# Two dense layers by Strassen's scheme, over 1024 rows and from weight sums kept in DRAM, with the stages in sequence

## The chip, the core and the metric

One NeuronCore of one Trainium2 chip runs the kernel. The metric is the device time of one launch in microseconds (us); the time of a kernel is the median of its runs. Five engines run their own queues in order: TensorE (PE in the profile; PEld is its loading of weights), VectorE (DVE), ScalarE (ACT), GpSimd (POOL), and SyncE (SP), which here only issues transfers between DRAM and SBUF. PSUM is the memory into which PE writes, in banks of 512 float32 per partition.

## What is computed

`x` holds 2048 rows of 576 float32. Two layers with the same weights: attention with learned features, then two dense layers with a squared ReLU between them (576 to 4608 to 576).

```python
q, k, v = heads(layernorm(x) @ wqkv)               # 32 heads of 18
phi_q = concat(softmax(q @ w_phi), softmax(-(q @ w_phi)))   # phi_k alike, per head
o = phi_q @ (phi_k.T @ v) / (phi_q @ phi_k.sum() + 1e-6)
x = x + o @ wo
h = relu(layernorm(x) @ w1 + b1) ** 2
x = x + h @ w2 + b2
```

Nothing in it is causal: the sums over the keys run over all 2048 rows, so no row's attention can end before every row's keys are done. Both kernels keep float32 accuracy in the large products by splitting each operand into a high and a low part (float32r) and adding three products of parts; `w_phi` is folded into `wqkv`.

## The kernel before

The rows are cut into four blocks of 512. For a block, `g_mlp` runs over 36 chunks of 128 hidden features. A chunk's slices of w1 and w2 are loaded from the inputs (288 KB each, and again for each block and layer), rounded to their high parts on ACT (L588, L591) and their low parts taken on DVE (L589, L592; a rest of 64 columns on POOL, L593). Fourteen products of 512 columns make the chunk's hidden rows in one PSUM bank (L605); ACT applies the bias, ReLU and square (L611, L612), DVE splits the result (L615, L616), and fourteen more products add to the output, which stays in five PSUM banks over all 36 chunks (L634, L627). The second products of a chunk are issued a step after its hidden ones, so that PE has work while ACT and DVE make the operands.

Attention is written as generators. `weave` takes one step of the dense layers of a block, then a step or two of the attention of the next block (`g_back`: norm, projections, softmax, the features over their denominators, the attention's output, its norm). The steps stand in this order in the program, and a list scheduler fixes from it the order of each engine's queue. Attention's own operations: max and min per head (L353, L354), two subtractions, one on DVE (L357) and one on POOL (L358), exp (L359), sums and reciprocals (L361, L362); for keys a product on POOL (L369). For queries `g_phi` takes the denominators: a product by the sums of the keys (L493), its sum per head (L494), a reciprocal (L497), a product (L501). `g_out` transposes the features (L521), splits them (L522, L523), multiplies by the key sums (L535), splits the result (L537, L539), multiplies by `wo` (L558) and adds to the rows (L561). `g_norm` is L245 to L278.

Two stretches in each layer have no dense products to weave with: the first layer's keys (with the fold before them), and the barrier, where the last keys end the sums and one block's attention runs alone before its dense layers can start.

Of the kernel before, what the change touches and what calls it, by code (L numbers as in the profile page):

```python
# [14 lines left out]
TB = 512  # L15
NT = TB // P
# [5 lines left out]
def layers_kernel(  # L22
# [24 lines left out]
    NB = S // TB  # L47
    NF = F // P
    KC = D // P                      # full blocks of 128 features
    DT = D - KC * P                  # the features beyond  # L50
    assert DT * 2 == P
# [4 lines left out]
    gw = [min(GW, D - g * GW) for g in range(NG)]  # L56
    HP = D // 2                      # 288

    cst = ctx.enter_context(tc.tile_pool(name="cst", bufs=1))
    sb = ctx.enter_context(tc.tile_pool(name="sb", bufs=2))  # L60
    ps_w = ctx.enter_context(tc.tile_pool(name="ps_w", bufs=2, space=bass.MemoryType.PSUM))
    ps_a = ctx.enter_context(tc.tile_pool(name="ps_a", bufs=1, space=bass.MemoryType.PSUM))
    dram = ctx.enter_context(tc.tile_pool(name="dram", bufs=1, space=bass.MemoryType.DRAM))

    xs = [[dram.tile([P, D], F32, name=f"xs{b}_{t}") for t in range(NT)] for b in range(NB)]
    xm = [[dram.tile([P, D], F32, name=f"xm{b}_{t}") for t in range(NT)] for b in range(NB)]
    xth = [dram.tile([P, NC * TB], F32, name=f"xth{b}") for b in range(NB)]
    xtl = [dram.tile([P, KC * TB], F32, name=f"xtl{b}") for b in range(NB)]
    wf = dram.tile([D, 2 * D], F32, name="wf")

    # Work tiles in PSUM: two banks at all times; the banks of the dense layers too while these rest.
    spare = {"tags": [], "i": 0}

    def wtile(name):
        n = len(spare["tags"])
        spare["i"] += 1
        i = spare["i"] % (n + 2)
        if i < n:
            return ps_a.tile([P, TB], F32, tag=spare["tags"][i], name=name)
        return ps_w.tile([P, TB], F32, tag="w", name=name)  # L80

    def drain(gen):
        for _ in gen:
            pass

    def weave(main, other, rate):
        """main's steps with other's between them, rate of these to one; then the rest of other."""
        due = 0.0
        for _ in main:
            due += rate  # L90
            while due >= 1.0 and next(other, other) is not other:
                due -= 1.0
        drain(other)

    def lagged(n, produce, consume):
        """consume(i, produce(i)) for all i, each a step behind, so that no engine waits for the other."""
        held = None
        for i in range(n):
            new = produce(i)
            if i:  # L100
                consume(i - 1, held)
            held = new
            yield
        consume(n - 1, held)
        yield

# [17 lines left out]
    zeros = zero.unsqueeze(1).to_broadcast([1, TB // P, P])  # L124
    mhalf = cst.tile([P, 1], F32, name="mhalf")
    nc.vector.memset(mhalf, -0.5)
    b1t = cst.tile([P, NF], F32, name="b1t")
# [6 lines left out]
    def rows_twice(src, c0, n):  # L134
        """The last DT rows of src, columns c0.., on both halves of the partitions."""
        w = src.shape[1]
        return bass.AP(tensor=src.tensor, offset=src.offset + KC * P * w + c0,
                       ap=[[0, 2], [w, DT], [1, n]])

    TAGS_A = ("whi", "wlo")  # L140
    TAGS_B = ("s2", "h1")

# [1 line left out]
    def g_fold(kpair):  # L144
        """Makes wf, and of it the pieces for k at once."""
        phi = sb.tile([P, NC, P], F32, tag="r1", name="phi")[:GW, :NG, :GW]
# [7 lines left out]
        raws, folds = {}, {}  # L154

        def turn(k):
            c, i = divmod(k, 3)
            if i == 0:
                raws[c] = sb.tile([P, 2 * D], F32, tag="E", name=f"fr{c}", bufs=4)
                nc.sync.dma_start(raws[c], wqkv[c * P : (c + 1) * P, : 2 * D] if c < KC  # L160
                                  else rows_twice(wqkv, 0, 2 * D))
                folds[c] = sb.tile([P, 2 * D], F32R, tag="hb", name=f"ff{c}").bitcast(F32)
            w, n = gw[batches[i][0][1]], len(batches[i])
            pt = wtile(f"fp{c}_{i}")
            for j, (h, g) in enumerate(batches[i]):
                a = h * D + g * GW
                nc.tensor.transpose(pt[:w, j * P : (j + 1) * P], raws[c][:, a : a + w], ident)
            wt = sb.tile([P, TB], F32, tag="hr", name=f"ft{c}_{i}", bufs=2)
            nc.vector.tensor_copy(wt[:w, : n * P], pt[:w, : n * P])
            return wt  # L170

        def times(k, wt):
            c, i = divmod(k, 3)
            w, n = gw[batches[i][0][1]], len(batches[i])
            folded = folds[c]
# [4 lines left out]
            keys = []  # L180
            if i < 2:
                nc.scalar.activation(folded[:, i * D : i * D + n * w], po[:, : n * w], AF.Copy)
                if i == 1:
                    keys = [(0, 0, HP, 0), (1, 0, n * w - HP, HP)]
            else:
                nc.scalar.activation(folded.rearrange("p (h d) -> p h d", h=2)[:, :, last * GW :],
                                     po[:, : 2 * w].rearrange("p (h d) -> p h d", h=2), AF.Copy)
                keys = [(1, last * GW - HP, w, w)]
            for half, to, width, at in keys:
                hi, lo = (piece[:, c, to : to + width] for piece in kpair[half])  # L190
                nc.scalar.activation(hi, po[:, at : at + width], AF.Copy)
                nc.vector.tensor_sub(lo, po[:, at : at + width], hi.bitcast(F32))
            if i == 2:
                m = P if c < KC else DT
                nc.sync.dma_start(wf[c * P : c * P + m, :], folded[:m])

        yield from lagged(3 * NC, turn, times)

# [1 line left out]
    def piece_tiles(name, tags):  # L200
        return [sb.tile([P, NC * HP], F32R, tag=tag, name=f"{name}{n}").rearrange("p (c n) -> p c n", c=NC)
                for tag, n in zip(tags, "hl")]

    def wpiece(src, c0, name, tags=TAGS_A, heads=False):
# [13 lines left out]
        for p, c in parts:  # L218
            nc.scalar.activation(hi[p, c], raw[p, c], AF.Copy)
            nc.vector.tensor_sub(lo[p, c], raw[p, c], hi[p, c].bitcast(F32))  # L220
# [596 lines left out]
```

## Time and profile before

| what | value |
|---|---|
| time, median of 3 runs | 2693.22 us (2692.66 to 2694.44) |
| profiled execution, first to last instruction | 2693.9 us |
| busy: PE, DVE, ACT, POOL | 2614.6, 1574.4, 1065.3, 605.8 us |
| products and transposes on PE | 13364 |
| mean granted clock of PE | 0.989 |
| DRAM traffic | 280.26 MB, 104 GB/s over the span |
| instructions | 36380 |

The profile gives, for one execution, each engine's busy time; the 40 equal slices of the span (busy tenths, the clock granted to PE in tenths, DMA share); the chain of work that ended last; and groups of instructions by line, engine and shape with their busy time, the mean length of one in ns, and the idle time before them with what ended it. A window gives the busy times of a stretch. Lengths of PE's products overlap, since they are pipelined; the step from one to the next is read from starts.

### The profile page before, as it was taken

What the parts mean: (1) busy time and instruction counts of PE and PEld (TensorE: products, weight loads), DVE (VectorE), ACT (ScalarE), POOL (GpSimd) and SP (SyncE); (2) the same over time, 40 slices, a digit from 0 to 9 for tenths busy, and PEclk for the clock granted to TensorE, in tenths of its full rate; (3) what the DMA queues carried; (4) which work ended last, traced back from release to release, by engine and by line L of the source; (5) the groups of instructions that cost most, each with busy time, mean ns of one, the idle gap of its engine ahead of it and who ended that gap; (6) DMA issues with size and microseconds to landing.
All of it is one profiled execution on the core that took longest, in us unless ns stands there. A gap on an engine that the chain in (4) does not pass through costs nothing. (4 is left out here: it accounts for less than half of the span.)

```text
span 2693.9 us, 36380 instructions
## 1 busy us (share of the span) xinstructions
PE 2614.6 (97%) x13364; PEld 2211.8 (82%) x13364; DVE 1574.4 (58%) x2561; ACT 1065.3 (40%) x1837; POOL 605.8 (22%) x647
## 2 busy tenths in 40 slices
PE   6998999999999999999999989999999999999998
PEld 5997788888878888788888977888888887888887
DVE  5668944365764567547544688444854476444343
ACT  3334343344433444434443333434434343433433
POOL 1443411112311123112211333111321123111110
PEclk8998999999999999999999989999999999999999
DMA  6211233352333532334333113333432343234332
GB/s 208 89 32 45 74 110 101 98 180 84 109 112 97 171 110 82 112 97 132 113 95 109 43 57 114 87 100 102 154 118 86 102 160 97 84 101 128 98 97 74
DMA packets 289021, 280.26 MB, mean 104 GB/s; under 512 B 18697, under 2 KB 230153, under 8 KB 286793
## 3 DMA queue, kind: packets, MB, share of 16 engines
q1 hardware_dynamic: 288841, 277.92, 34.0%
q8 instruction: 105, 1.72, 0.3%
q14 instruction: 75, 0.61, 0.1%
HBM read 246.90 MB, written 30.97 MB: 103 GB/s over the span
## 5 line engine op out<-in xcount | busy, mean ns | idle before, releaser
L605 PE MATMUL m_0ph<-a_0nh,m_0h 128*128 128x512 f32 (+1 forms) x760 | 231.6, 387 | 0.0
L605 PE MATMUL m_2ph<-a_2nh,m_2h 128*128 128x512 f32 (+1 forms) x760 | 228.2, 383 | 0.1
L634 PE MATMUL m_3acc<-m_3s,m_3hb 128*128 128x512 f32 x864 | 214.2, 395 | 3.0 <-DVE m_3hb L616 1.8
L634 PE MATMUL m_0acc<-m_0s,m_0hb 128*128 128x512 f32 x864 | 214.7, 395 | 2.5 <-DVE m_0hb L616 1.1
L634 PE MATMUL m_1acc<-m_1s,m_1hb 128*128 128x512 f32 x864 | 213.3, 394 | 2.6 <-DVE m_1hb L615 1.8
L634 PE MATMUL m_2acc<-m_2s,m_2hb 128*128 128x512 f32 x864 | 213.2, 394 | 0.9 <-DVE m_2hb L615 0.7
L634 PEld LDWEIGHTS m_0acc<-m_0s,m_0hb 128*128 128x128 f32 x864 | 161.0, 188 | 43.4 <-DVE m_0hb L616 4.2
L634 PEld LDWEIGHTS m_3acc<-m_3s,m_3hb 128*128 128x128 f32 x864 | 160.9, 188 | 43.1 <-DVE m_3hb L616 4.2
L634 PEld LDWEIGHTS m_1acc<-m_1s,m_1hb 128*128 128x128 f32 x864 | 161.3, 188 | 42.1 <-DVE m_1hb L615 3.2
L634 PEld LDWEIGHTS m_2acc<-m_2s,m_2hb 128*128 128x128 f32 x864 | 161.3, 188 | 40.3 <-DVE m_2hb L615 2.2
L605 PEld LDWEIGHTS m_0ph<-a_0nh,m_0h 128*128 128x128 f32 x760 | 141.0, 190 | 28.5 <-DVE m_0h L589 0.4
L605 PEld LDWEIGHTS m_2ph<-a_2nh,m_2h 128*128 128x128 f32 x760 | 139.6, 188 | 28.8 <-DVE m_2h L589 1.0
L589 DVE TENSOR_TENSOR m_2h<-m_2r,m_2h 128x640 fp32r<-128x640 f32 x72 | 61.5, 854 | 165.4 <-ACT m_2h L588 165.4
L589 DVE TENSOR_TENSOR m_1h<-m_1r,m_1h 128x640 fp32r<-128x640 f32 x72 | 61.0, 848 | 162.5 <-ACT m_1h L588 162.5
L589 DVE TENSOR_TENSOR m_3h<-m_3r,m_3h 128x640 fp32r<-128x640 f32 x72 | 60.8, 844 | 160.8 <-ACT m_3h L588 160.8
L589 DVE TENSOR_TENSOR m_0h<-m_0r,m_0h 128x640 fp32r<-128x640 f32 x72 | 62.7, 870 | 145.9 <-ACT m_0h L588 139.2
L593 POOL TENSOR_TENSOR m_3s<-m_3r,m_3s 128x64 fp32r<-128x64 f32 x72 | 57.3, 797 | 355.2 <-ACT m_3s L591 349.6
L593 POOL TENSOR_TENSOR m_2s<-m_2r,m_2s 128x64 fp32r<-128x64 f32 x72 | 55.9, 777 | 360.9 <-ACT m_2s L591 355.4
L593 POOL TENSOR_TENSOR m_1s<-m_1r,m_1s 128x64 fp32r<-128x64 f32 x72 | 58.0, 805 | 343.8 <-ACT m_1s L591 341.7
L593 POOL TENSOR_TENSOR m_0s<-m_0r,m_0s 128x64 fp32r<-128x64 f32 x72 | 53.3, 741 | 346.3 <-ACT m_0s L591 323.8
L611 ACT ACTIVATE m_0hr<-m_0ph,b1t 128x512 f32<-128x512 f32 x72 | 49.6, 689 | 193.9 <-PE m_0ph L605 184.7
L611 ACT ACTIVATE m_3hr<-m_3ph,b1t 128x512 f32<-128x512 f32 x72 | 49.7, 690 | 192.4 <-PE m_3ph L605 187.8
(1527 smaller groups left out, 6949.8 us busy)
## 6 DMA issues: line engine op xcount, KB each, us to landing
m_3r<-in_B_w SPq DMA_DIRECT2D x72, 288.0 KB
m_2r<-in_B_w SPq DMA_DIRECT2D x72, 288.0 KB
m_0r<-in_B_w SPq DMA_DIRECT2D x72, 288.0 KB
m_1r<-in_B_w SPq DMA_DIRECT2D x72, 288.0 KB
m_3r<-in_B_w SPq DMA_DIRECT2D x72, 256.0 KB
m_2r<-in_B_w SPq DMA_DIRECT2D x72, 256.0 KB
m_0r<-in_B_w SPq DMA_DIRECT2D x72, 256.0 KB
m_1r<-in_B_w SPq DMA_DIRECT2D x72, 256.0 KB
```

The lines of the kernel that those rows point to most:

```text
L589: nc.vector.tensor_sub(l1, r1, h1.bitcast(F32))
L593: nc.gpsimd.tensor_sub(s2[:, D : D + DT], r2[:, R:], s2[:, R:D].bitcast(F32))
L605: nc.tensor.matmul(ph[:, cols], a, m, start=(k == 0), stop=(k == 3 * KC + 1))
L611: nc.scalar.activation(hr, ph, AF.Relu, bias=b1t[:, f : f + 1])
L634: nc.tensor.matmul(acc[t], a[:, rows], m, start=(begin and k == 0), stop=(end and k == 2))
```

## The change

The dense layers work on superblocks of 1024 rows, two for each layer, and by Strassen's scheme in Winograd's form: rows, hidden features and model features are each cut in two, and seven products of half-size blocks stand for eight. The hidden layer takes a pair of chunks at a time (`NJ` = 18 pairs): seven products of weight sums with row sums, each seven matmuls of 512 columns (L585), over three PSUM banks, with additions on DVE (L603 to L618) that put together the four blocks of the result. The second layer takes two pairs of chunks at a time: for each of seven products, operands are made of the four hidden blocks (POOL, L631 to L637; split by ACT and DVE, L639, L640), and four tiles of 128 rows by 288 columns are made in PSUM, six matmuls each (L657), and added into SBUF (L661). At a superblock's end `combine` (L671 to L693) adds the seven results into four blocks and the rows.

The weight sums are made and split once and put into DRAM: `prep_w1` (L359 to L379), one pair of chunks with each tile of the first layer's keys and two more at its end; `prep_w2` (L381 to L399) in the first superblock's dense stage. The split projection weights go to DRAM too. `norm2` makes the seven row sums on POOL and splits them (L511 to L533).

`weave` is gone. Each layer is a stage of keys for all 16 tiles (norm, v, k and q, both softmaxes, the sums; the exponentials of q go to DRAM), and for each superblock `stage_q` (the rest of the attention) and `stage_mlp`.

```diff
+    def prep_w1(pl, j):
...
+        s4, s1, s2, s3 = ws[:, 2], ws[:, 4], ws[:, 5], ws[:, 6]
+        nc.gpsimd.tensor_add(s1, a21, a22)
+        nc.gpsimd.tensor_sub(s3, a11, a21)
+        nc.gpsimd.tensor_sub(s2, s1, a11)
+        nc.gpsimd.tensor_sub(s4, a12, s2)
+        wt = pl.tile([P, 7, 5, P], F32R, tag="wt", name=f"wt{j}")
+        nc.scalar.activation(wt[:, :, :3], ws[:, :7], AF.Copy)
+        nc.vector.tensor_sub(wt[:, :, 3:], ws[:, :7, :2], wt[:, :, :2].bitcast(F32))
...
+        nc.sync.dma_start(w1d[j], wt.rearrange("p a b c -> p (a b c)").bitcast(F32))
+
...
+            def hidden(j):
...
+                def product(p, bank, fresh):
+                    w = pl.tile([P, 5, P], F32R, tag="w1", name=f"{n}w{j}_{p}", bufs=6)
+                    nc.sync.dma_start(w.rearrange("p b m -> p (b m)").bitcast(F32),
+                                      w1d[j][:, p * 5 * P : (p + 1) * 5 * P])
+                    k = 0
+                    for l, r in ((0, 0), (0, 3), (3, 0), (1, 1), (1, 4), (4, 1), (2, 2)):
+                        nc.tensor.matmul(bank, w[:, l], X[:, p, r], start=(fresh and k == 0), stop=(k == 6),
+                                         skip_group_check=not fresh)
+                        k += 1
+
...
+                a, b, c = banks
+                product(0, a, True)
+                nc.scalar.activation(p1, a, AF.Copy)
+                product(5, b, True)
+                nc.vector.tensor_add(u2, b, p1)
+                product(1, a, False)
...
+            def operand(j, p):
...
+                nc.scalar.activation(t[:, 0], o[p], AF.Copy)
+                nc.vector.tensor_sub(t[:, 1], o[p], t[:, 0].bitcast(F32))
+                return t
+
...
+            def second(js, first, final):
+                for p in ORDER2:
+                    parts = []
+                    for j in js:
+                        w = pl.tile([P, 2, HP], F32R, tag="w2", name=f"{n}v{j}_{p}", bufs=5)
+                        nc.sync.dma_start(w.rearrange("p k n -> p (k n)").bitcast(F32),
+                                          w2d[j][:, p * 2 * HP : (p + 1) * 2 * HP])
+                        parts.append((operand(j, p), w))
+                    for t in range(4):
+                        rows = slice(t * P, (t + 1) * P)
+                        pt = wtile(f"{n}y{js[0]}_{p}{t}")[:, :HP]
+                        k, last = 0, 3 * len(parts) - 1
+                        for hl, w in parts:
+                            for x, y in ((0, 0), (0, 1), (1, 0)):
+                                nc.tensor.matmul(pt, hl[:, x, rows], w[:, y], start=(k == 0), stop=(k == last))
+                                k += 1
+                        to = acc[:, p, t]
+                        if not first:
+                            nc.vector.tensor_add(to, pt, to)
+                        elif p in (1, 3):
+                            nc.vector.tensor_add(to, pt, b2t[:, :HP])
...
+            hidden(1)
+            for g in range(NJ // G):
+                if prep:
+                    for j in range((g + 2) * G, min((g + 3) * G, NJ)):
+                        prep_w2(pl, j)
+                if (g + 1) * G < NJ:
+                    hidden((g + 1) * G)
+                second([g * G + k for k in range(G)], g == 0, g == NJ // G - 1)
+                if (g + 1) * G + 1 < NJ:
+                    hidden((g + 1) * G + 1)
+            combine()
...
-            weave(g_mlp(layer, b, ready, rows, f"m{n}"), g_back(), 1.0 if layer else 1.5)
...
+                xT = lead.pop(0)
+                vt = make_v(pl, xT, wts["v"], f"v{layer}{t}")
+                kraw = make_raw(pl, xT, wts["k"], f"k{layer}{t}")
+                qraw = make_raw(pl, xT, wts["q"], f"Q{layer}{t}")
+                if held:
+                    kv_tile(banks, *held, False)
+                held = (vt, soft_k(pl, kraw, f"K{layer}{t}"))
+                soft_q(pl, qraw, layer, t, f"s{layer}{t}")
+                if layer == 0:
+                    prep_w1(pl, t)
+                    if t >= NT - 2:
+                        prep_w1(pl, t + 2)
+            kv_tile(banks, *held, True)
+            kv_end(pl, layer, banks)
+        with pool(f"px{layer}") as px:
+            X = px.tile([P, 7, 5, TW], F32R, tag="X", name=f"X{layer}")
+            for sb in range(NSB):
+                if sb:
+                    X = px.tile([P, 7, 5, TW], F32R, tag="X", name=f"X{layer}{sb}")
+                stage_q(layer, sb, X)
+                stage_mlp(layer, sb, X)
```

Where instructions move, the order of the engines shows it. First VectorE in the first layer's keys. Before (`K_2_1` is a key tile, `n_3` the norm of the next block):

```order
170 L353 TENSOR_REDUCE K_2_1m<-k_2s_1490 128x32
171 L354 TENSOR_REDUCE K_2_1m<-k_2s_1490 128x32
172 L267 TENSOR_TENSOR n_3l<-n_3p_1538,n_3h 128x4x128
173 L357 TENSOR_TENSOR K_2_1e<-k_2s_1490,K_2_1m 128x576
174 L250 TENSOR_SCALAR n_3n_1641<-x_3_2_1631,n_3m_1634,n_3d_1635 128x512
175 L361 TENSOR_REDUCE K_2_1r<-K_2_1e 128x64
176 L362 RECIPROCAL K_2_1r<-K_2_1r 128x64
177 L353 TENSOR_REDUCE K_2_2m<-k_2s_1598 128x32
```

and after (`K010` and `s010` are the softmaxes of K and Q of tile 10, `wt` the split w1 sums):

```order
261 L266 TENSOR_REDUCE K010m<-k010s 128x32
262 L267 TENSOR_REDUCE K010m<-k010s 128x32
263 L270 TENSOR_TENSOR K010e<-k010s,K010m 128x576
264 L273 TENSOR_REDUCE K010r<-K010e 128x64
265 L274 RECIPROCAL K010r<-K010r 128x64
266 L375 TENSOR_TENSOR wt_2499<-ws_2486,wt_2499 128x7x256
267 L266 TENSOR_REDUCE s010m<-Q010s 128x32
268 L267 TENSOR_REDUCE s010m<-Q010s 128x32
```

A key tile's softmax stood next to the norm of a later block; now the split of the w1 sums (L375), which waits for ACT and POOL, stands between the softmax of K and that of Q.

Second, VectorE in the dense layers. Before, in the first chunks of a block (`m_0h`, `m_0s` split weights, `m_0hb` the split hidden rows):

```order
1866 L589 TENSOR_TENSOR m_0h_2_16850<-m_0r_2_16845,m_0h_2_16850 128x640
1867 L615 CAST m_0hb_16724<-m_0hr_16721 128x512
1868 L616 TENSOR_TENSOR m_0hb_16724<-m_0hr_16721,m_0hb_16724 128x512
1869 L589 TENSOR_TENSOR m_0h_3_16930<-m_0r_3_16925,m_0h_3_16930 128x640
1870 L615 CAST m_0hb_16744<-m_0hr_16741 128x512
1871 L616 TENSOR_TENSOR m_0hb_16744<-m_0hr_16741,m_0hb_16744 128x512
1872 L592 TENSOR_TENSOR m_0s_2_16853<-m_0r_2_16846,m_0s_2_16853 128x512
```

and after, inside the second layer of a superblock (`m11hl` the split operands, `m11acc` the seven results in SBUF, `m11y` a tile in PSUM):

```order
2896 L640 TENSOR_TENSOR m11hl_4_25296<-m11s_25248,m11hl_4_25296 128x512
2897 L661 TENSOR_TENSOR m11acc<-m11y_60_25262,m11acc 128x288
2898 L640 TENSOR_TENSOR m11hl_4_25301<-m11s_25256,m11hl_4_25301 128x512
2899 L661 TENSOR_TENSOR m11acc<-m11y_61_25270,m11acc 128x288
2900 L661 TENSOR_TENSOR m11acc<-m11y_62_25278,m11acc 128x288
2901 L661 TENSOR_TENSOR m11acc<-m11y_63_25286,m11acc 128x288
2902 L640 TENSOR_TENSOR m11hl_5_25339<-m11s_25248,m11hl_5_25339 128x512
2903 L661 TENSOR_TENSOR m11acc<-m11y_40_25304,m11acc 128x288
```

Splitting of weights is gone from the stream; in its place stand the additions of PSUM tiles, four for each of the seven products, with the next product's operands split between them.

Third, TensorE. Before, in the dense layers (`m_2` is a block's dense layers, `v_3` the v projection of another block's keys):

```order
2306 L308 MATMUL v_3pv_5600<-w_3v1h,n_3h 128x288
2307 L308 MATMUL v_3pv_5600<-w_3v1l,n_3h 128x288
2308 L605 MATMUL m_2ph_5630<-a_2nh,m_2h_5_5623 128x512
2309 L605 MATMUL m_2ph_5630<-a_2nl,m_2h_5_5623 128x512
2310 L605 MATMUL m_2ph_5630<-a_2nh,m_2h_5_5623 128x512 x2
2311 L605 MATMUL m_2ph_5630<-a_2nl,m_2h_5_5623 128x512
```

and after, at the end of the first superblock's dense stage (`m00y` its last output tiles, `q_0apt` the transposes of the next stage's attention):

```order
1204 L657 MATMUL m00y_22_9048<-m00v_2_9020,m00hl_2_9023 128x288 x3
1205 L657 MATMUL m00y_22_9048<-m00v_2_9026,m00hl_2_9029 128x288 x3
1206 L657 MATMUL m00y_23_9056<-m00v_2_9020,m00hl_2_9023 128x288 x3
1207 L657 MATMUL m00y_23_9056<-m00v_2_9026,m00hl_2_9029 128x288 x3
1208 L451 MATMUL q_0apt_9202<-ident,q_00e 126x128
1209 L451 MATMUL q_0apt_9211<-ident,q_00e 126x128
```

Where projections of another block stood between two chunks, the dense products now run to their end, and the next superblock's attention begins behind them.

More of the change, by code (lines that the diff above doesn't have):

```diff
@@ L63, in layers_kernel @@
+    psa = ctx.enter_context(tc.tile_pool(name="psa", bufs=1, space=bass.MemoryType.PSUM))
     dram = ctx.enter_context(tc.tile_pool(name="dram", bufs=1, space=bass.MemoryType.DRAM))
[L65 to L68, printed above, removed]
@@ L69, in layers_kernel @@
-    wf = dram.tile([D, 2 * D], F32, name="wf")
-    spare = {"tags": [], "i": 0}
-    def wtile(name):
[L75 to L93, printed above, removed]
@@ L189, in times @@
[L189 to L202, printed above, removed]
@@ L314, in make_v @@
+    def make_v(pl, xT, w, name):
+        vt = pl.tile([P, NG, GW + 1], F32, tag="v", name=f"{name}v", bufs=3)
         nc.gpsimd.memset(vt[:, :, 0:1], 1.0)
[L315 to L328 removed]
@@ L398, in kv_tile, with kv_begin, bank_view @@
+    def kv_begin(layer):
+        banks = [abank(i, f"kv{layer}{i}") for i in range(len(pairs))]
+        for pt, gs in zip(banks, pairs):
+            m = gw[gs[0]] + 1
+            nc.tensor.matmul(pt[:m], zero[:, :m], zeros, start=True, stop=False)
+        return banks
+    def bank_view(pt):
+        return pt[: GW + 1, : 4 * GW].rearrange("p (g s f) -> p g s f", g=2, s=2)
+    def kv_tile(banks, vt, e, last):
+        for pt, gs in zip(banks, pairs):
+            po = bank_view(pt)
             for g in gs:
```

919 lines of the change are left out of this document (414 added, 505 removed).

## Prediction

> **What bounds the kernel now.** I read the page first (busy shares, the 40 slices), then the chain of waits, then windows over single stages, then the groups by shape for the price of each operation. The page:
>
> ```profile
> span 2693.9 us, 36380 instructions
> PE 2614.6 (97%) x13364; PEld 2211.8 (82%) x13364; DVE 1574.4 (58%) x2561; ACT 1065.3 (40%) x1837; POOL 605.8 (22%) x647
> PEclk8998999999999999999999989999999999999999
> ```
>
> TensorE (PE) is busy for 97% of the span at full clock nearly throughout; VectorE (DVE) has 42% to spare. The span is 0.7 us over the median of the runs (2693.22), so a sum against the span needs no correction. The chain gives the pace of the products:
>
> ```profile
> 2366.12 3.98 PE a_2po L558 x30
> 2370.11 3.18 PE m_3ph L605 x14
> ...
> 2404.96 3.17 PE m_3ph L605 x14
> 2408.14 2.79 PE m_3acc L634 x12
> 2410.93 0.47 PE m_3acc L627 x2
> 2411.39 3.26 PE m_3ph L605 x14
> ```
>
> From 2404.96 to 2411.39 there are 28 products of 512 columns, 0.230 us each; from 2366.12 to 2370.11 there are 30 of 288 columns, 0.133 each. (The durations in the groups overlap; these are the steps from one to the next.) The windows tell what each stage is like, columns as headed: length, busy time of PE, PEld, DVE, ACT, POOL, clock, DMA share, GB/s:
>
> ```profile
> 0.00:52.80 52.80, 29.84 (x175) 25.72 (x176) 29.59 (x72) 16.59 (x35) 5.50 (x22) 0.81 0.58 207
> 30.00:45.00 15.00, 6.59 (x28) 5.93 (x29) 8.14 (x16) 6.35 (x13) 0.19 (x1) 0.50 0.58 212
> 52.80:61.40 8.60, 8.60 (x67) 8.60 (x67) 4.46 (x14) 2.88 (x12) 2.15 (x5) 1.00 0.94 218
> 140.70:181.00 40.30, 40.30 (x288) 39.29 (x287) 23.83 (x31) 14.25 (x35) 15.87 (x13) 1.00 0.06 15
> 235.00:301.00 66.00, 57.32 (x371) 51.46 (x370) 61.11 (x110) 25.00 (x45) 26.94 (x27) 0.91 0.16 51
> 500.00:700.00 200.00, 198.62 (x1029) 168.66 (x1028) 115.33 (x180) 84.66 (x147) 39.10 (x46) 1.00 0.44 134
> ```
>
> In the woven part (500 to 700) PE is full while DVE does 115 of 200 us: the attention of the next block rides under the dense products. Where attention stands alone (235 to 301, four tiles of 128 rows of the barrier) DVE is busy 61.1 of 66 us and PE's clock falls to 0.91. So attention by itself is paced by DVE, and the weave is what hides that. The change takes the weave away; that decides my forecast.
>
> **The products: the gain.** Before: 36 chunks x 28 x 4 blocks x 2 layers = 8064 products of 512 columns, x 0.230 = 1855 us. After: four superblock stages of 18 x 49 = 882 hidden products of 512 (3528, 811 us) and 18 x 84 = 1512 second products of 288 (6048, 804 us): 1615. PE's work falls by 240 us. "TensorE: Matmul & The Clock Gate" of the Trainium skill (section "Back-to-back issue gap") gives N/2.4 + 2.5 ns, which is 216 and 122.5 ns, and would put these products at 1502 us as an estimate; the measured steps above are longer, and decide.
>
> **The second layer's additions.** Its output no longer gathers in PSUM: per pair of chunks DVE adds 28 tiles of 288 into SBUF and splits 14 operands of 512. The nearest rows:
>
> ```profile
> L616 DVE TENSOR_TENSOR m_1hb<-m_1hr,m_1hb 128x512 fp32r<-128x512 f32 x72 | 51.9, 720 | 2.2
> L592 DVE TENSOR_TENSOR m_0s<-m_0r,m_0s 128x512 fp32r<-128x512 f32 x72 | 60.2, 837 | 36.0 <-ACT m_0s L591 34.1 <-DMA m_0r<-in_B_w 1.9
> L561 DVE TENSOR_TENSOR a_2x<-a_2po,a_2x 128x288 f32<-128x288 f32 x16 | 7.3, 457 | 11.2 <-PE a_2po L558 11.1
> L267 DVE TENSOR_TENSOR n_3l<-n_3p,n_3h 128x512 fp32r<-128x512 f32 x8 | 5.5, 687 | 0.6 <-ACT n_3h L266 0.5
> ```
>
> 168 products take PE 22.4 us. By the order of the changed kernel 28 additions and 11 of the splits stand beside them: 28 x 0.457 + 11 x 0.72 = 20.7 us, about 22 with some 0.03 us between instructions: a tie with PE. The other 3 splits and the 10 additions of 512 (about 0.69 by L267) lie under the two hidden groups (2 x 49 x 0.230 = 22.5 us) with room. A pair costs PE 45.0 us; I take 46.5, one and a half for the tie. Bounds 45 (PE alone) and 50 (splits at L592's price and POOL's four combinations per chunk in the way). Nine pairs, four stages: 1674 us, from 1620 to 1800. That the weights come split from DRAM takes ACT and DVE work off (L588, L589, L592); it buys nothing by itself, since it lay under PE. The loads, 295 or 328 KB for each 1.6 us of PE, need some 200 GB/s; 218 is shown at a share of 0.94 in the window from 52.8, with smaller packets. I cost them at nothing, because five or six buffers run ahead; uncovered, they are in the upper bound.
>
> **First layer's keys, with the preparation of w1.** Before, a tile of keys took 40.3 / 4 = 10.1 us, PE full. After, Q's projections and softmax join each tile, and one of 18 preparations of w1. Its tiles are single, and in DVE's order its split (L375) stands between K's and Q's softmax; on POOL the product that normalises K's features stands ahead of three of the preparation's four sums. So a tile is one chain through three in-order queues. The rows for it:
>
> ```profile
> L494 DVE TENSOR_REDUCE a_2u<-a_2m 128x32 f32<-128x576 f32 x16 | 11.6, 733 | 0.0
> L357 DVE TENSOR_TENSOR K_1e<-k_0s,K_1m 128x576 f32<-128x576 f32 x1 | 1.4, 1398 | 0.0
> L357 DVE TENSOR_TENSOR K_2e<-k_1s,K_2m 128x576 f32<-128x576 f32 x1 | 0.8, 842 | 0.0
> L361 DVE TENSOR_REDUCE K_2r<-K_2e 128x64 f32<-128x1152 f32 x3 | 4.0, 1350 | 0.1
> L362 DVE RECIPROCAL K_2r<-K_2r 128x64 f32<-128x64 f32 x3 | 1.7, 553 | 0.0
> L220 DVE TENSOR_TENSOR a_0q0l<-a_0q0r,a_0q0h 128x1440 fp32r<-128x1440 f32 x1 | 1.7, 1659 | 0.6 <-ACT a_0q0h L219 0.6
> L588 ACT ACTIVATE m_2h<-m_2r 128x640 fp32r<-128x640 f32 x72 | 52.5, 729 | 3.7 <-DMA m_2r<-in_B_w 3.6
> L359 ACT ACTIVATE K_2e<-K_2e 128x1152 f32<-128x1152 f32 x3 | 3.5, 1169 | 0.7 <-DVE K_2e L357 0.7
> L593 POOL TENSOR_TENSOR m_3s<-m_3r,m_3s 128x64 fp32r<-128x64 f32 x72 | 57.3, 797 | 355.2 <-ACT m_3s L591 349.6 <-issue 5.6
> L369 POOL TENSOR_TENSOR K_2e<-K_2e,K_2r 128x1152 f32<-128x1152 f32 x3 | 6.5, 2154 | 3.9 <-DVE K_2r L362 3.9
> ```
>
> A softmax is max and min (2 x 0.73), the subtraction (1.4), exp (1.17), sum (1.35), reciprocal (0.55): 5.9 us, for K and Q 11.8. Between them: POOL's product 2.15; three sums of 384, between 0.8 (64 wide) and 1.2 (on the line from 64 to 1152), I take 1.0: 3.0; ACT's rounding of 2688 elements, on the line through 640 and 1152, 2.5; L375, 1792 wide, 2.0 by L220's price for an element. That is 9.7. One of the two small splits L378 (896 wide, 1.05 by the same price) shows, the other lies under Q's exp; a dozen hand-offs between engines at some 0.1 make 1.4. Together 24 us a tile; 20 if the sums overlap K's product and a hand-off is free, 26 with all POOL work at its slower price. On SP the store of each prepared tile waits for that DVE work, with later loads behind it; x has three buffers, which cover it. 16 x 24 = 384, plus a start like the 52.8 us of before (50, as one tile is normed ahead instead of four), plus 35 for two preparations left over and the sums' end: 469 (395 to 521).
>
> **Second layer's keys.** No preparation: 84 projections x 0.133 + sums and transposes, 13 us of PE a tile, against 12 of DVE by the same rows with the norm's. Close enough to collide: 14.5. 16 x 14.5 = 232, plus some 30 before the first tile is through, for three weights, 8.8 MB together, that SP issues only behind the previous stage's stores (at the 218 GB/s of the window from 52.8 they take 41; PE's first tile wants the last of them only after some 9): 262 (240 to 290).
>
> **The attention alone, four times.** Per tile on DVE: two reductions 1.46, one product of 576, two and a half splits of 512 from PSUM 1.7, the output's splits 0.9, two additions 0.9, statistics and norm 2, half of the operands' split (1792 and 896 wide) 1.5, the small ones 1.3:
>
> ```profile
> L501 DVE TENSOR_TENSOR a_0Q0e<-a_0Q0e,a_0Q0r 128x576 f32<-128x576 f32 x2 | 3.4, 1721 | 0.0
> L501 DVE TENSOR_TENSOR a_2Q1e<-a_2Q1e,a_2Q1r 128x576 f32<-128x576 f32 x2 | 2.9, 1428 | 0.0
> ```
>
> With 1.5 for the product: 11.3 us, so 90 for eight tiles. Nothing hides the head (loads behind the stores of the stage before, then POOL's products) nor the tail (four POOL combinations, a rounding, two splits, ahead of the first hidden product): 8 and 10. With another 10 for waits in order, 118 a stage, 472 for four; bounds 98 (no waits, half of the ends hidden) and 140 (the 15 us a tile of the barrier window, and the ends). Q's features go through DRAM, 0.62 MB a tile; I cost that at nothing, since three and four buffers let it run ahead (at 218 GB/s it is 2.9 us a tile; uncovered, it is in the upper bound).
>
> **The rest.** Combining a superblock: 32 additions of 288 on DVE, 14.6 us, all ahead of the next stage's first DVE instruction: 55 for the four (40 to 75; some lie under the last products). w2's preparation in the first stage alone: 36 halves with single tiles on POOL and DVE (about 2 us of DVE per chunk, in a tie already): 50 (15 to 110).
>
> **Sum**: 469 + 262 + 472 + 1674 + 55 + 50 = 2982 us, 288 over the span.
>
> **The rivals.** (1) *The engines overlap as before; the end is faster.* The queues would run far enough ahead of each other for PE to set the pace in keys and attention too. What is not dense products costs 2694 - 1855 = 839 us now; with 1620, combination 55 and 50 of preparation that is 2565. For it: the 40.3 us of keys with PE full. Against it: the barrier window, where the same attention left PE 9 us idle in 66. It decides if a first-layer keys tile takes under 14 us and an attention stage under 75. Half-way mixtures are still over 2694: the keys and the attention would have to give back 288 of 469 + 472 us. Chance 0.07.
>
> (2) *The second layer is set by DVE and POOL.* If POOL's combinations block DVE, 28 additions cost not 0.457 but about 0.76 (the ratio of L357's 1398, beside POOL's L358, to its 842): 8.4 us a pair, 36 pairs, 300 more: 3282. Against it: L561's 16 calls average 457, as its other groups do. "SBUF — State Buffer" of the Trainium skill (section "Who interferes with whom") says that a VectorE instruction with at most one SBUF input does not contend with GpSimd, one with two does; by that the additions from PSUM are safe and only the splits suffer, as L561 and L357 have it. Chance 0.12.
>
> (3) *The clock.* In 30 to 45 us, with PE busy 6.6 of 15, the clock is 0.50. With PE idle half of a tile in the first keys and a third of the attention, its bursts would run at half speed: PE's 13 us a tile then become up to 26, over the chain's 24 (+32), and attention tiles go from 11 to about 14 (+95): 3110. "TensorE: Matmul & The Clock Gate" of the Trainium skill (section "What's actually happening") has the clock halved after an idle window of about 3.4 us and freed after as long a busy one; bursts here are longer than that, so by the rule they lose 1.7 us each and hardly the whole. Chance 0.07, inside the range.
>
> **How the numbers follow.** The forecast has 0.74. Its terms' bounds, taken as independent, give -130 and +180 (roots of the summed squares): 2850 to 3160. With half-way mixtures below and rival 3 above, the range is 2835 to 3165; left out are rival 1, most of 2, and the forecast's tails. A measurement here tells 0.2% from no change. Slower: the forecast, 2, 3, less 0.02 of low mixtures: 0.91; within 0.2%: 0.02; faster: 0.07.
>
> **What would show it.** In the changed profile: PE near 85% of the span or under it, the clock under 0.95; the dense stages near 46.5 us a pair with PE over 95%; keys of layer 0 near 24 us a tile with PE half idle, waiting behind the chain POOL, ACT, DVE; attention stages near 118 with DVE about 80% busy. It is wrong if dense pairs take over 50 us (rival 2), if PE stays over 95% in the keys (rival 1), or if PE's step there is 0.27 us (rival 3).

## The result and the profile after

The changed kernel takes 3233.77 us (median of 4 runs, 3230.2 to 3235.85), the kernel before 2693.83 beside it: a ratio of 1.2002, 95% interval 1.1985 to 1.2019. Slower, as forecast, but by 540 us and not by 288: the time lies 69 us over the top of the range.

The page of the changed kernel (span and busy times, the clock in 40 slices, the traffic):

```profile
span 3234.1 us, 40986 instructions
PE 2519.0 (78%) x14892; PEld 2284.1 (71%) x14892; DVE 1947.1 (60%) x3239; ACT 1133.3 (35%) x1871; POOL 1014.0 (31%) x975
PEclk9777677679999996889999799967999996799999
DMA packets 309697, 552.48 MB, mean 171 GB/s; under 512 B 31849, under 2 KB 145465, under 8 KB 305913
```

PE was busy for 97% of the span and is for 78%; the traffic has doubled, mostly by the preparation, the reading of prepared weights and Q's features. The clock in the slices shows the stages: 9 where dense products run, 6 to 8 where attention stands alone. The windows of the changed kernel by stage (length, then busy times of PE, PEld, DVE, ACT, POOL, clock, DMA share, GB/s):

```profile
68.80:309.10 240.30, 131.78 (x795) 125.26 (x794) 120.09 (x165) 58.88 (x96) 80.62 (x81) 0.76 0.42 147
309.10:525.60 216.50, 117.81 (x688) 112.19 (x687) 94.87 (x118) 50.96 (x82) 65.64 (x59) 0.73 0.36 124
591.00:715.50 124.50, 76.74 (x488) 69.28 (x488) 85.47 (x152) 36.12 (x54) 60.78 (x60) 0.76 0.31 108
715.50:1237.00 521.50, 448.68 (x2394) 384.38 (x2394) 311.38 (x495) 219.68 (x340) 189.10 (x222) 0.95 0.77 244
1237.00:1264.00 27.00, 0.00 (x0) 0.00 (x0) 11.58 (x29) 0.00 (x0) 1.97 (x2) 0.55 0.82 281
1264.00:1392.00 128.00, 80.02 (x488) 71.96 (x488) 84.30 (x150) 33.58 (x52) 55.51 (x56) 0.73 0.27 99
1392.00:1803.30 411.30, 407.91 (x2397) 370.08 (x2397) 261.01 (x459) 184.62 (x304) 107.50 (x82) 0.99 0.63 189
1803.30:1857.70 54.40, 14.05 (x84) 13.49 (x84) 24.13 (x63) 3.24 (x9) 6.89 (x17) 0.59 0.70 266
1857.70:2090.00 232.30, 215.18 (x1509) 207.94 (x1508) 178.03 (x240) 79.18 (x171) 94.53 (x81) 0.98 0.15 53
```

Two of these are as foreseen: a dense stage without preparation (1392 to 1803) is 411 us with PE at 99%, and the second layer's 16 key tiles (1857.7 to 2090) take 14.5 us each. The first layer's keys (the first two rows) are not: 15 tiles from 68.8 to 525.6, 31 us each in the steady part, with no engine busy for more than 55% of the time. The same stretch read as a chain of waits, tile 8 (SPq is SyncE's own queue: the issue of a transfer; rows under 0.1 us are left out):

```profile
305.34 1.10 DVE wt L378
306.46 0.56 DVE s07e L274
307.08 0.33 SPq L289
...
307.58 1.02 SPq L364
308.65 1.22 SPq L366
...
314.65 1.78 SPq L364
316.47 1.06 SPq L366
...
317.64 3.07 DMA n014x<-in_A_x
320.71 0.98 POOL ws L370
...
325.89 0.99 POOL ws L372
326.92 2.45 ACT wt L374
329.39 2.02 DVE wt L375
```

From L370 on it is the chain that I had priced, at the prices I had given it. What stands ahead of it is not in my sum: the slices of w1 for the next pair can be loaded only when the last reader of the single buffer is done (L378, at 306.4), and in SyncE's queue they stand behind the store of Q's features (L289), which waits for L274 until 307.0. Then eight issues on SyncE take 10 us, and the landing 3 (its row has the name of x's load, which was issued right behind). Over the whole stretch from 68.8 to 525.6 the issues L364 and L366 hold 21% of this chain and the landing of w1's slices 14%, together 160 us. Against the 24 us of the forecast the loop is 31.

### The profile page after: what moved, and what is told of

It reads as the page before. It is cut to its first block, busy times and chain, and to the rows that moved or that the text cites. A ratio compares the mean times of both kernels' runs of the same rounds, so it can differ in the third digit from the quotient of the medians.

```text
span 3234.1 us, 40986 instructions
## 1 busy us (share of the span) xinstructions
PE 2519.0 (78%) x14892; PEld 2284.1 (71%) x14892; DVE 1947.1 (60%) x3239; ACT 1133.3 (35%) x1871; POOL 1014.0 (31%) x975
## 4 chain that ended last, share of the span: by engine, by line
PE 46%; DVE 16%; DMA 10%; POOL 10%; ACT 6%; SPq 6%; issue 5%; POOLq 0%; DVEq 0%; ACTq 0%
PE m01h L585 6%; PE m10h L585 6%; PE m11h L585 6%; PE m11y L657 6%; PE m01y L657 6%; PE m10y L657 5%; PE m00h L585 3%; DMA ws<-in_B_w 2%; SPq L364 2%; PE m00y L657 2%; SPq L389 2%; DMA m00w<-w1d 2%; SPq L366 1%; ACT wt L374 1%; DMA q_00e<-eqd 1%
## 5 line engine op out<-in xcount | busy, mean ns | idle before, releaser
L585 PE MATMUL m00h<-X,m00w 128*128 128x512 f32 x882 | 230.6, 421 | 50.6 <-DMA m00w<-w1d 32.3
L585 PEld LDWEIGHTS m00h<-X,m00w 128*128 128x128 f32 x882 | 175.5, 202 | 102.7 <-issue 31.8
L657 PE MATMUL m00y<-m00v,m00hl 128*128 128x288 f32 x1512 | 221.1, 304 | 32.6 <-DVE m00acc L661 21.1
L657 PEld LDWEIGHTS m00y<-m00v,m00hl 128*128 128x128 f32 x1512 | 209.5, 193 | 44.9 <-DVE m00acc L661 26.5
L585 PE MATMUL m01h<-X,m01w 128*128 128x512 f32 x882 | 204.9, 393 | 12.1 <-ACT X L531 10.9
L585 PE MATMUL m10h<-X,m10w 128*128 128x512 f32 x882 | 204.1, 392 | 12.1 <-ACT X L531 10.9
L585 PE MATMUL m11h<-X,m11w 128*128 128x512 f32 x882 | 204.1, 392 | 12.1 <-ACT X L531 10.9
L657 PE MATMUL m01y<-m01v,m01hl 128*128 128x288 f32 x1512 | 205.0, 296 | 2.1 <-DVE m01hl L640 1.8
L657 PEld LDWEIGHTS m01y<-m01v,m01hl 128*128 128x128 f32 x1512 | 202.9, 190 | 4.4 <-DVE m01hl L640 2.3
L657 PE MATMUL m10y<-m10v,m10hl 128*128 128x288 f32 x1512 | 203.9, 295 | 2.5 <-DVE m10hl L640 1.8
L657 PE MATMUL m11y<-m11v,m11hl 128*128 128x288 f32 x1512 | 203.9, 295 | 2.1 <-DVE m11hl L640 1.8
L657 PEld LDWEIGHTS m10y<-m10v,m10hl 128*128 128x128 f32 x1512 | 201.4, 188 | 5.1 <-DVE m10hl L640 2.3
L657 PEld LDWEIGHTS m11y<-m11v,m11hl 128*128 128x128 f32 x1512 | 201.7, 188 | 4.6 <-DVE m11hl L640 2.3
L585 PEld LDWEIGHTS m01h<-X,m01w 128*128 128x128 f32 x882 | 167.2, 190 | 47.5 <-ACT X L531 11.3
L585 PEld LDWEIGHTS m10h<-X,m10w 128*128 128x128 f32 x882 | 166.7, 190 | 47.2 <-ACT X L531 11.3
L585 PEld LDWEIGHTS m11h<-X,m11w 128*128 128x128 f32 x882 | 166.6, 190 | 47.2 <-ACT X L531 11.3
L375 DVE TENSOR_TENSOR wt<-ws,wt 128x1792 fp32r<-128x1792 f32 x18 | 36.4, 2024 | 162.3 <-ACT wt L374 162.3
L661 DVE TENSOR_TENSOR m10acc<-m10y,m10acc 128x288 f32<-128x288 f32 x224 | 94.1, 447 | 13.1 <-PE m10y L657 12.2
L661 DVE TENSOR_TENSOR m11acc<-m11y,m11acc 128x288 f32<-128x288 f32 x224 | 93.9, 447 | 12.4 <-PE m11y L657 11.6
```

Source lines behind the costliest of these rows:

```text
L375: nc.vector.tensor_sub(wt[:, :, 3:], ws[:, :7, :2], wt[:, :, :2].bitcast(F32))
L585: nc.tensor.matmul(bank, w[:, l], X[:, p, r], start=(fresh and k == 0), stop=(k == 6), skip_group_check=not fresh)
L657: nc.tensor.matmul(pt, hl[:, x, rows], w[:, y], start=(k == 0), stop=(k == last))
L661: nc.vector.tensor_add(to, pt, to)
```

## The experiments

All times below stand beside 3233.77 of the changed kernel and 2694 of the one before. A preparation left out means that 17 of 18 pairs read the first pair's prepared weights.

**Two theories for the first keys.** Theory R: the reload is part of the loop. Theory C, rival 3 of the prediction in these keys: PE's projections at half clock set the tile. The first run takes w1's preparation away:

```diff
-                if layer == 0:
-                    prep_w1(pl, t)
...
+                if layer == 0 and t == 0:
+                    prep_w1(pl, t)
```

> Leaves out 17 of the 18 preparations of w1: one pair is prepared, and all pairs read it, so the dense layers compute with one pair's w1. Theory R (reload): a tile of the first keys takes 31 us because the next pair's w1 slices are reloaded into the single buffer only when its last reader is done; without the preparation a tile takes 15 to 16 us, the stage falls from 591 to about 340, the time to about 2980 us. Theory C (clock): the tile is set by TensorE's projections, which run at half clock between gaps (84 x 0.267 = 22 us); a tile stays at 22 or more and the time at about 3100.

Measured: 2956.46 us, ratio 1.0968 (1.0918 to 1.1018). The tiles' exponentials of K start at 90.8, 105.3, 119.8 and so on to 291.4: 14.3 us a tile, as in the second layer. In that stretch:

```profile
90.80:291.40 200.60, 190.41 (x1354) 185.16 (x1355) 159.10 (x213) 70.09 (x152) 82.81 (x73) 0.99 0.15 56
```

PE is at 95% and the clock at 0.99: the low clock of the first keys followed from the gaps and did not make them. Theory C falls. What the low clock adds to a tile's chain was not tried apart; PE's rows are some 2% of the changed kernel's chain from 68.8 to 525.6. w1's preparation costs 277 us, of which I had some 150 in the tiles (16 times 24 less 14.5) and up to 35 behind them. For each of the 17 preparations left out that is 16.3 us, against the 9.5 of the forecast. The next two runs change the reload and leave the work as it is. First the order of issue, the next pair's loads ahead of the stores:

```diff
+        if j + 1 < NJ:
+            load_w1(pl, j + 1)
         nc.sync.dma_start(w1d[j], wt.rearrange("p a b c -> p (a b c)").bitcast(F32))
...
```

> Computes all. The eight loads of the next pair are issued on SyncE ahead of the stores of the prepared pair and of Q's features instead of behind them. Theory R with a backlog: an issue takes 1.0 to 1.8 us because 2.8 MB of stores stand ahead of it in the transfer queues; ahead of them it takes 0.4 to 0.5, the eight 4 us instead of 10, a tile 24 to 25 us, the time about 3135. Theory R without backlog (the issue costs that much by its number of pieces): a tile 30 to 31, the time 3220 to 3234. Theory C: no change.

Measured: 3179.26 us, ratio 1.1795 (1.1746 to 1.1843): 54 us less, about half of what I expected. The issues, in the changed kernel and then in this one (shortest/median/longest in ns):

```profile
L364 SPq DMA_DIRECT2D ws<-in_B_w x72: 379/1248/1891, 29.7 to 558.7; - x72
L366 SPq DMA_DIRECT2D ws<-in_B_w x72: 553/994/10632, 30.2 to 559.8; - x72
```

```profile
L364 SPq DMA_DIRECT2D ws<-in_B_w x72: 366/472/1841, 29.0 to 473.5; - x72
L366 SPq DMA_DIRECT2D ws<-in_B_w x72: 558/559/6742, 29.5 to 474.0; - x72
```

By the medians the same transfers are issued in 0.47 and 0.56 us when these stores do not stand ahead of them, and in 1.25 and 0.99 behind 2.8 MB of stores. A preparation now comes every 24.7 us (ScalarE's roundings of w1 stand from 87.96 to 483.77, 16 steps), but a tile, for which I had expected 24 to 25, still takes 30.6 (exponentials of K from 131.17 to 468.11, 11 steps): the scheduler runs preparations ahead of the tiles, and only the last tiles are quick. So the time tells more than the pace: 223 us over the run without preparation, or 13.1 for each of the 17. Then a second buffer:

```diff
-        ws = pl.tile([P, 8, 3, P], F32, tag="ws", name=f"ws{j}")
+        ws = pl.tile([P, 8, 3, P], F32, tag="ws", name=f"ws{j}", bufs=2)
...
```

> Computes all. Two buffers for the w1 slices, so that a reload can run a tile ahead; the scheduler orders the queues anew by it. Theory R: what is left is the chain of two softmaxes and POOL, ACT, DVE work that the prediction priced at 24 us; a tile takes 22 to 25, the time is 3110 to 3140. Theory C, or a chain that does not hang on the loads: a tile stays at 29 to 31, the time over 3200.

Measured: 3140.17 us, ratio 1.165 (1.158 to 1.1719): 94 us less. A preparation comes every 20 us (82.75 to 403.54, 16 steps); a tile takes 31 until they are done (exponentials of K from 96.61 to 377.71, 9 steps) and some 14 after, so the tile is as slow as theory C wanted, but the time is at the top of R's range and far under C's. It is 184 us over the run without preparation, 10.8 for each of the 17. From 16.3 through 13.1 to 10.8 against 9.5 forecast: theory R holds, and the reload was most of what the step in the prediction lacked. What sets the stretch now was not found; VectorE is busy for only 64% of it:

```profile
96.60:403.00 306.40, 174.18 (x975) 165.06 (x975) 196.04 (x207) 83.94 (x123) 140.02 (x117) 0.77 0.51 180
```

**The first dense stage.** It is 110 us longer than the others. Without w2's preparation, by the same kind of edit:

> Leaves out 17 of the 18 preparations of w2; all pairs read one pair's w2. If the first dense stage is 110 us longer than the other three (521 against 411) for the preparation alone, it falls to 411 to 415 and the time to about 3125. Rival: part of it is something else of the first stage (its weights have just been written); then it stays over 440 and the time over 3150.

Measured: 3127.66 us, ratio 1.1603 (1.155 to 1.1656), 106 us less; the stage falls from 521 to 422. That is a little over the 411 to 415 expected. So w2's preparation costs some 100 us, twice what I gave it. What of it? Three runs:

```diff
-            ws = pl.tile([P, 8, W], F32, tag="pf", name=f"v{j}_{h}")
+            ws = pl.tile([P, 8, W], F32, tag="pf", name=f"v{j}_{h}", bufs=2)
...
-                    x = pl.tile([P, 2, D], F32, tag="pf" if t % 2 else "po", name=f"{n}x{t}")
+                    x = pl.tile([P, 2, D], F32, tag="pf" if t % 2 else "po", name=f"{n}x{t}", bufs=2 if t % 2 else 1)
```

> Computes all. Two buffers for the w2 slices (not for the split result, for which there is no room). Theory S (SyncE's queue): in the first dense stage SyncE stands waiting for the preparation's last reader with the products' weights behind it; with the slices loaded a half ahead this falls by a third or more, the stage from 521 to 470 to 490, the time to 3185 to 3205. Theory T (transfers: share 0.8 there) or V (VectorE's and GpSimd's work): under 10 us, 3225 to 3240.

Measured: 3209.29 us, ratio 1.1911 (1.1887 to 1.1935): 24 us less. That is under what theory S wanted and over what its rivals did, and not all of it is w2's: the same buffers serve the rows in `combine`. The first dense stage falls by 14 us (520.8 to 506.6, first to last product), and the four combinations, 13.8 to 15.3 us each from the last product to the last addition, take 11.0 to 11.3, some 14 less together; other stretches gave a few back. Then the work of POOL and DVE taken out:

```diff
-            nc.gpsimd.tensor_sub(t1, b12, b11)
...
-            nc.vector.tensor_sub(wt[:, :, 1], ws[:, :7], wt[:, :, 0].bitcast(F32))
+            for k in range(2):
+                nc.scalar.activation(wt[:, 0:3, k], ws[:, 0:3], AF.Copy)
...
```

> Leaves out w2's sums and their split: what is loaded is copied by ScalarE alone into the tile that is stored, so the second layer computes with other numbers; loads, stores and buffers stay. Theory V: the 110 us are VectorE's 2 us a chunk and GpSimd's sums in a stage that ties already; without them the stage falls under 450, the time under 3165. Theory S or T: the stage keeps over 480, the time over 3190; between the two, 3165 to 3190, both have a part.

Measured: 3203.58 us, ratio 1.189 (1.1866 to 1.1914): 30 us less, the stage 490. The engines' work, which is where I had put the cost, is less than a third of it. Last, the stores:

```diff
+            n = 1 if j else 7
-            nc.sync.dma_start(d4[:, :, :, h * W : (h + 1) * W], wt.bitcast(F32))
+            nc.sync.dma_start(d4[:, :n, :, h * W : (h + 1) * W], wt[:, :n].bitcast(F32))
...
```

> Leaves out six sevenths of the stores of the prepared w2, for all pairs but the first, and the second layer reads the first pair's weights for six of seven products; loads, sums, splits and buffers stay. Theory T: the first dense stage is held by its transfers (share 0.81, 255 GB/s, some 31 MB of these stores in pieces of 576 bytes); without them the stage falls from 521 to under 460, the time under 3175. Theory S with V (waits of SyncE's queue and VectorE's work, 22 and 31 us by the runs before): it keeps over 490, the time over 3205; between, both.

Measured: 3181.16 us, ratio 1.1802 (1.1767 to 1.1836): 53 us less, the stage 469, between the two expectations, so neither theory has it alone. In the first dense stage the three take 14, 31 and 52 us off, near the 99 of the run without preparation; whether they add was not tried. What PE waited for in that stage of the changed kernel (total us, times, longest):

```profile
PE m00h L585 <- DMA m00w<-w1d: 32.3, 17, 3.4
PE m00y L657 <- DVE m00acc L661: 21.1, 20, 2.2
PE m00y L657 <- DMA m00v<-w2d: 5.6, 8, 2.1
```

Weights for the products come late, and so do the additions. Without the stores PE's two waits for weights fall to 3.3 and 5.0 us; with the second buffer they do not (35.4 and 13.9). SyncE's waits for the split result, which has one buffer in all these runs, were not tried apart. The wait for L661 falls under 1.4 us in both the run without the splits and the run with the second buffer.

**Would it win if the preparation were free?**

> Leaves out 17 of the 18 preparations of w1 and of w2, so the dense layers compute with one pair's weights. If preparation were free, would the change win? Theory: no. The two savings add up (3234 - 277 - 106 = 2851, between 2835 and 2865), and what is left over the kernel before, some 155 us, is the attention that nothing hides, less what the products save. Rival: the preparations share a cost or cover one another (the first dense stage gains from what the keys leave); then it is off 2851 by more than 20.

Measured: 2855.08 us, ratio 1.0594 (1.0569 to 1.062). The two add up (2851), and the kernel is still slower by 161 us. What remains is the unwoven attention. To price that by itself I undid the weave in the kernel before, and nothing else:

```diff
-        due = 0.0
-        for _ in main:
-            due += rate
...
+        drain(main)
         drain(other)
```

> Computes all. The kernel before with its weave undone: a block's dense layers run to their end, then the next block's attention. No Strassen, no preparation. Theory: the weave hides 150 to 300 us of attention that VectorE and the hand-offs pace, about what Strassen's products save; 2850 to 3000. Rival: the attention is paced by TensorE wherever it stands (839 us of it now), and the weave hides only its ends: 2700 to 2780.

Measured: 3060.43 us, ratio 1.1356 (1.1329 to 1.1384): the weave is worth 366 us, more than I had expected. A block's dense layers and the attention behind them in that kernel:

```profile
602.50:852.90 250.40, 245.15 (x1078) 201.13 (x1079) 107.51 (x180) 94.92 (x150) 36.17 (x48) 0.97 0.35 101
852.90:1024.00 171.10, 102.49 (x572) 86.48 (x570) 93.20 (x145) 41.81 (x79) 40.80 (x33) 0.78 0.22 73
```

Alone, the attention between two blocks (with keys of the second layer) takes 171 us with no engine over 60%. The chain of waits in it passes from engine to engine: about 66 us of VectorE, 57 of TensorE, 17 of ScalarE, 16 of GpSimd and 10 of transfers. So no one engine sets its pace; what the clock of 0.78 adds there was not tried. With this the 540 us divide: 366 for the weave, -205 for all the rest of the change once its weights are there (2855 against 3060), 379 for making those weights (3234 against 2855). The middle term is not Strassen's products alone: weights that come split, larger blocks and Q's features through DRAM are in it too, and no run takes them apart.

**The ends of the stages.** From the last addition of `combine` to the first hidden product, a later attention stage takes 141 us (1251 to 1392), where I had 118. The chain at its head and at its tail, second stage of the first layer (rows under 0.1 us are left out here too):

```profile
1251.53 0.90 SPq L544
1252.48 0.81 SPq L545
1253.34 10.41 DMA q_00e<-eqd
1264.04 1.23 POOL q_00m L427
...
1356.00 3.85 PE q_21po L498 x29
1359.85 0.34 PE q_1np L521 x3
1360.27 1.26 ACT q_1nr L523 x3
...
1366.28 2.46 ACT X L531
...
1378.45 2.45 ACT X L531
1380.93 2.03 DVE X L532
...
1389.55 2.45 ACT X L531
1392.03 2.04 DVE X L532
```

13 us pass until the first features have landed, behind the other loads; and after the attention's last products (1360) three pairs of tiles go one by one through POOL's sums, ACT's rounding and DVE's split, 34 us. I had 8 and 10. With the sums on VectorE:

```diff
-        nc.gpsimd.tensor_sub(t1, b12, b11)
+        nc.vector.tensor_sub(t1, b12, b11)
...
```

> Computes all. The four sums of the seven row operands are made on VectorE instead of GpSimd, where they take 1.0 us each. Theory of the ends: an attention stage is long for its head and tail; in the tail the chain of two pairs' norms shortens by 2 us each, 4 to 5 a stage, 3214 to 3226 in all. Rival: VectorE sets the stage's pace (85 of 128 us busy), and 2 us more a pair make it 8 longer a stage: 3250 to 3270.

Measured: 3208.3 us, ratio 1.1898 (1.1875 to 1.1922), 25 us less. The first stage goes from 124.5 to 114.7, from 592.0 to 706.7: 10 us, twice what I expected, and the rival (VectorE as the bound) falls: it had room. The four stages gain 39 us together in the traces (9.8, 12.5, 7.9 with the second layer's keys, and 8.8); the dense stages gave some 11 of it back, 8 of them the first. Why they did was not tried.

The second layer's keys start late too; the chain there has one row for it, and the edit calls `norm1` of tile 1 ahead of the weights:

```profile
1818.85 23.61 DMA n11x<-xs
```

```diff
             lead = [norm1(pl, layer, 0, f"n{layer}0")]
+            if layer:
+                lead.append(norm1(pl, layer, 1, f"n{layer}1"))
...
```

> Computes all. In the second layer the rows of tile 1 are loaded ahead of the three projection weights, not behind them. Theory: the second layer's keys start late because TensorE's first projections stand behind the transposes of tile 1, whose rows wait 23.6 us behind 8.8 MB of weights; the first softmax comes some 15 to 20 us earlier, the time falls to 3214 to 3220. Rival: the wait moves on to the weights themselves (K's weights land no earlier); then under 5 us.

Measured: 3216.7 us, ratio 1.1936 (1.1906 to 1.1966), 17 us less; the first exponential of K stands at 1844.2 and not 1859.5. In the new chain the same wait, 25.77 us, is tile 2's, no longer ahead of the first projections.

**All that computes the whole, together** (two buffers for w1 and for w2, tile 1 first, sums on VectorE):

> Computes all. Four edits together: two buffers for the w1 slices (94 us alone), tile 1's rows ahead of the second layer's weights (17), the row sums on VectorE (25), two buffers for the w2 slices (not measured yet; 0 to 40). If they add up: 3234 - 136 - (0 to 40) = 3058 to 3098. Still slower than the kernel before by 13 to 15%, since none of them covers the attention.

Measured: 3074.86 us, ratio 1.142 (1.1401 to 1.1439). The four add up (3234 - 94 - 17 - 25 - 24 = 3074). No version that I found beats the kernel before.

## Why the prediction was wrong

The sign held, and so did its reason, attention that nothing hides; the size failed. By the prediction's own terms, in us:

| term | forecast | measured | from |
|---|---|---|---|
| first layer's keys | 469 | 591 | start to the first feature product |
| second layer's keys | 262 | 295 | 1816.5 to 2111.5 |
| attention, four times | 472 | 536 | 124.5 + 141 + 129 + 141 |
| dense products | 1674 | 1656 | 3 x 411.3 + 422 |
| preparation of w2 | 50 | 100 | 521.5 - 422 |
| combining | 55 | 56 | four times 13 to 16 |

The terms measured sum to 3234. Two lie beyond the bounds that the prediction gave them: the first layer's keys by 70 us (521) and the second's by 5 (290).

- *The products* were right: 45.7 us a pair (411.3 / 9), between PE's 45.0 and the 46.5 taken. The tie with VectorE did not bind; VectorE is busy 261 of 411 us. Rival 2 fell: the additions L661 take 447 ns, against 457 for L561 before. The splits of GpSimd's sums take 1.04 us, against 0.77 for the others, and that is hidden. The Trainium skill ("SBUF — State Buffer", section "Who interferes with whom") says that a VectorE instruction with at most one SBUF input, outside the two-port modes, does not contend with GpSimd, and that one with two SBUF inputs contends with a GpSimd instruction that reads SBUF. The trace agrees: in the last dense stage a split (two SBUF inputs) takes 0.68 us when GpSimd is idle and 1.05 to 1.27 on average with GpSimd at work beside it, while an addition L661 (one) takes 0.45 to 0.46 either way. The groups of the changed kernel by shape:

```profile
L661 DVE TENSOR_TENSOR m11acc<-m11y,m11acc 128x288 f32<-128x288 f32 x224 | 93.9, 447 | 12.4 <-PE m11y L657 11.6
L640 DVE TENSOR_TENSOR m11hl<-m11s,m11hl 128x512 fp32r<-128x512 f32 x54 | 56.2, 1043 | 5.2 <-ACT m11hl L639 5.2
L640 DVE TENSOR_TENSOR m11hl<-m11a,m11hl 128x512 fp32r<-128x512 f32 x72 | 54.9, 772 | 3.6 <-ACT m11hl L639 3.6
```

- *The first keys: the step that failed.* "Together 24 us a tile" priced every instruction rightly and closed the loop at the wrong place. It gave the reload of the single w1 buffer no term ("x has three buffers, which cover it" spoke of x alone), and it let no issue on SyncE cost anything. The reload is some 13 us (307.6 to 320.7): issues that are slow behind stores, and the landing. Half of it lies beside K's softmax (307.8 to 314.0), which 24 had counted; the rest makes 31. Of the 122 us that this term lacks, the 15 steps have 97 (457 against 360), the start 19 (69 against 50) and the end 6 (65 against 59). `a_w1_once`, `b_load_first` and `c_ws_two` show the reload from three sides.
- *w2's preparation* was given to VectorE's tie; the runs put half of it on the stores (52 us), 31 on GpSimd's and VectorE's work and 14 on the single buffer. The traffic was costed at nothing for the steady stages, rightly (a share of 0.63), but the first stage has the stores besides, and stands at 0.77.
- *The attention alone*: the 90 us for eight tiles agree with VectorE's 84 to 85 busy. But that attention is "paced by DVE", as I read the barrier window, did not hold: VectorE is busy for 60 to 69% of these stages and not for 80, and more work on it (`g_sums_dve`) made them shorter. The ends were sized by one chain each (8 and 10); they are 13 for loads, some 11 more until the first transposes, and 34, since the norms of three pairs queue up behind each other.
- *Second layer's keys*: 14.5 us a tile as said; the start was 41 and not 30, since PE's order puts tile 1's transposes ahead of tile 0's projections, and 21 at the end (the sums' end, and loads until the first feature product) were not in the sum.
- *Rival 1* was far off. *Rival 3*, the clock: the windows show 0.73 to 0.76 in those stages, as that rival wanted, but with the gaps gone the clock came back and the tile went to PE's own pace. Whether it costs something in the attention stages was not tried apart.
- *The range* took the terms' errors as independent. They were not, as I read them: chains through several queues were priced too short in several places at once, each time at their ends or at a reload.

## What to carry to other kernels

Before counting what fewer products save, price what they were hiding: undoing the weave alone costs more here (366 us) than the rest of the change with free weights gives back (205). In a loop on a single buffer, write down the whole circle, the reload with its issues and landing too, and look at what stands ahead of those issues in the queue. At the border of a stage, count pairs that go one after the other, not one chain.

## What the hardware showed that I had not expected

The issue of a transfer on SyncE is not a constant: 0.47 us (median) with its loads ahead of the stores, 1.25 behind 2.8 MB of stores, for the same 128 KB. And attention alone fills no engine: 171 us with TensorE busy 60% and VectorE 54% of it.
